# Queries by kv as four float32 products in the quarters of the array, from the fifth chunk on

## The chip, the cores and the metric

The kernel runs on one core of one Trainium2 chip. Its time is the device time of one execution in microseconds (us). Less is better.

## What is computed

Linear attention over 8 batches, 8 heads, 576 tokens and 64 dimensions a head, and a gated feed-forward layer behind it. q is drawn with a spread of 0.8, k with 0.32, v with 0.1.

```python
q_s = exp(q - max(q, axis=-1));  q_s /= sum(q_s, axis=-1) + 1e-9      # over the head's 64 dimensions
k_s = exp(k - max(k, axis=2));   k_s /= sum(k_s, axis=2) + 1e-9       # over the 576 tokens
kv  = einsum('bhsd,bhse->bhde', k_s, v)                               # 64 x 64 for each head
x   = einsum('bhsd,bhde->bhse', q_s, kv)                              # queries by kv
x   = x.transpose(0, 2, 1, 3).reshape(4608, 512)                      # tokens x (heads * 64)
out = ((x @ w_a) * (x @ w_b)) @ w_out                                 # 512 -> 1536 -> 512
```

## The kernel before, in words

The 4608 tokens are worked in nine chunks of 512 (`T`, index `c` from 0). A batch has 576 tokens, so a batch ends within most chunks. While the feed-forward layer of chunk `c` runs on TensorE, the attention of chunk `c + 1` is worked in between. So the queries of the fifth chunk (`c` = 4) are worked during the feed-forward of the fourth.

**Feed-forward.** `x @ w_a` and `x @ w_b` are formed by seven products of blocks instead of eight (Strassen's scheme in Winograd's form). Each float32 operand is split into two float32r parts, high and low, and each product is high by high, high by low and low by high. One call of `product` (L835) issues 12 matmuls of 256 columns into a two-bank tile of PSUM: `kx` (bank pair tag k0), `ky` and later `kp` (tag k1), `ka` (tag k2). VectorE and ScalarE join the results (L1443 to L1481). `project` (L864) multiplies the gated result by `w_out`: 12 matmuls of 512 columns a call, into `po`.

**Attention.** The eight heads are four pairs (`g`); a pair fills the 128 partitions, 64 of each head. For each batch and two pairs, `kv_two` takes the softmax of k times v by plain float32 products (`pk`, L582): each head writes one half of the columns of the array, with all 128 rows; ten products to a pair. Then `kv_two` scales them, masks what is between two heads, and splits the block-diagonal 128 x 128 matrix into two float32r parts `kvh` and `kvl`.

For the queries, `q_stats` takes the maximum and the sum of each token and head, which go through a transposition (`pst`, L686) and through memory and come back as rows along the tokens (`q_rows`, tile `mr`). `q_turned` loads q with its dimensions on the partitions (`qtt`). `q_exp` (L721) adds the maximum's row on VectorE (L722), takes the exponential on ScalarE (L723), and splits it into `qh` on ScalarE (L341) and `ql` on VectorE (L344). `x_product` (L752) multiplies by kv: three float32r products of all 512 columns into one bank (tag `at`), or six where a batch ends within the chunk (L761). VectorE multiplies by the row of the reciprocal sums (L960) and writes `xf`, the input of the feed-forward.

**The order.** Up to the third chunk a table by hand (`ORDER`) gives each engine's order. From there on a scheduler places the instructions, with what `attend` hands it at three calls for each of six pairs of blocks; calls may be pinned behind a named instruction. `attention_tasks` (L914) makes the list of steps that those calls take.

**The end.** `store` (L871) copies each 128 x 512 block of results from PSUM, on VectorE and ScalarE in turn in the last chunk, and SP issues one DMA for each.

Of the kernel before, what the change touches and what calls it, by code (L numbers as in the profile page):

```python
# [7 lines left out]
F32 = mybir.dt.float32  # L8
# [247 lines left out]
def linear_attention_then_gated_ffn(  # L256
# [40 lines left out]
    TT = T // P  # L297
    NCH = NT // T
    LATE = NCH - qt_late.shape[0]

    const = ctx.enter_context(tc.tile_pool(name="const", bufs=1))
    sb = ctx.enter_context(tc.tile_pool(name="sb", bufs=2))
# [35 lines left out]
    def split(hi, lo, src, hi_engine="act"):  # L338

        if hi_engine == "act":  # L340
            nc.scalar.copy(out=hi, in_=src)  # L341
# [273 lines left out]
    def kv_two(b, g, kts, vts, tag):  # L615

        pk = ps.tile([P, 2, D + 1], F32, name="pk", tag=tag)
        for n in range(2):
            kv_sums(kts[n], vts[n], tag, pk[:, n])
        den = sb.tile([P, 2], F32, name="den2")  # L620
        nc.vector.tensor_scalar_add(den, pk[:, :, D], EPS)
        nc.vector.reciprocal(out=den, in_=den)
        kv = sb.tile([P, 2, P], F32, name="kv2", bufs=1)
        for n in range(2):
            nc.vector.scalar_tensor_tensor(
                out=kv[:, n].rearrange("p (h d) -> p h d", h=2),
                in0=pk[:, n, 0:D].unsqueeze(1).broadcast_to([P, 2, D]), scalar=den[:, n:n + 1],
                in1=mask.rearrange("p (h d) -> p h d", h=2), op0=ALU.mult, op1=ALU.mult,
            )
        split(*kv_home(b, g), kv, "dve")  # L630


    wholes = sb.tile([P, 2, NP, P], F32, name="wholes", tag="mr", bufs=2)
# [32 lines left out]

    def q_stats(qt, st):
        qv = qt.rearrange("p j h d -> p h j d")  # L670
        nm, rs = st[:, :, 0], st[:, :, 1]
        nc.vector.tensor_reduce(out=nm, in_=qv, axis=AX.X, op=ALU.max, negate=True)  # L672
        for h in range(2):
            for j in range(TT):
                nc.scalar.activation(  # L675
                    out=qt[:, j, h], in_=qt[:, j, h], func=AF.Exp, bias=st[:, h, 0, j:j + 1],
                    accum_out=st[:, h, 1, j:j + 1],
                )
        nc.vector.tensor_scalar_add(rs, rs, EPS)
        nc.vector.reciprocal(out=rs, in_=rs)  # L680

    def q_stats_out(c, st):

        n = NP * 2 * 2 * TT
        pst = ps.tile([n, P], F32, name="pst", tag="at")
        nc.tensor.transpose(pst, st.rearrange("p g h w j -> p (g h w j)"), ident)  # L686
# [3 lines left out]
        nc.sync.dma_start(out=dq, in_=sst)  # L690
        return dq.rearrange("(g h w j) p -> g h w (j p)", g=NP, h=2, w=2)

    def roomy(c):
        return c > LATE

# [23 lines left out]
    def q_exp(c, qt, rows):  # L721
        nc.vector.tensor_tensor(out=qt, in0=qt, in1=rows[0], op=ALU.add)  # L722
        nc.scalar.activation(out=qt, in_=qt, func=AF.Exp)  # L723
        if roomy(c):
            hl = sb.tile([P, 2, T], F32R, name="qhl", tag="mr", bufs=2)
            qh, ql = hl[:, 0], hl[:, 1]
        else:
            qh = sb.tile([P, T], F32R, name="qh", bufs=1)
            ql = sb.tile([P, T], F32R, name="ql", bufs=1)
        split(qh, ql, qt)  # L730
        return qh, ql
# [10 lines left out]
    def x_whole(c, g, qw, tag):  # L742
# [6 lines left out]
            nc.tensor.matmul(px[:, s], whole[b, g], qw[:, s], start=True, stop=True)  # L749
        return px  # L750

    def x_product(c, g, qhl, tag="at"):  # L752
        qh, ql = qhl
        t0 = c * T
        b0, b1 = t0 // S, (t0 + T - 1) // S
        n0 = min(T, (b0 + 1) * S - t0)
        px = ps.tile([P, T], F32, name="px", tag=tag)
        for b, s in ((b0, slice(0, n0)), (b1, slice(n0, T)))[:b1 - b0 + 1]:
            kvh, kvl = kvs[b, g]
            for i, (w, m) in enumerate(((kvh, qh), (kvh, ql), (kvl, qh))):  # L760
                nc.tensor.matmul(px[:, s], w, m[:, s], start=(i == 0), stop=(i == 2))  # L761
        return px
# [108 lines left out]
    def store(c, po):  # L871
        for t in range(TT):
            ot = sb.tile([P, DM], F32, name="ot", tag="wr", bufs=4)
            if c == NCH - 1 and t % 2 == 0:
                nc.vector.tensor_copy(out=ot, in_=po[t])
            else:
                nc.scalar.copy(out=ot, in_=po[t])
            nc.sync.dma_start(out=out[c * T + t * P:c * T + (t + 1) * P, :], in_=ot)
# [39 lines left out]
    def attention_tasks(c):  # L918

        xfs[c] = sb.tile([P, NP, T], F32, name="xf", bufs=1)  # L920
        steps = key_steps(range(c * T // S, (c * T + T - 1) // S + 1))
        if c == 2:
            steps = [(tasks[8][4],)] + steps
            steps[0] += tuple(lambda g=g: kv_split_whole(1, g) for g in range(NP))
            for g in (1, 2, 3):
                load, soft, turn, back, prod = late_key_task(g, "at")
                steps.append((
                    load, lambda soft=soft, turn=turn: (soft(), turn()),
                    lambda back=back, prod=prod: (back(), prod()),
                ))  # L930
        stats, last, turned, rows = [], [], [], []
        every = {}
        for g in range(NP):
            box = {}

            def a0(g=g, box=box):
                if g == 0:
                    every["st"] = sb.tile([P, NP, 2, 2, TT], F32, name="st", bufs=1)
                box["q"] = q_load(c, g)

            def a1(g=g, box=box):
                q_stats(box["q"], every["st"][:, g])
# [12 lines left out]
            def b1(box=box):  # L955
                box["e"] = q_exp(c, box["q"], box["r"])

            def b2(g=g, box=box):
                px = x_product(c, g, box["e"])
                nc.vector.tensor_tensor(out=xfs[c][:, g], in0=px, in1=box["r"][1], op=ALU.mult)  # L960

            turned.append(t0)
            rows.append(r0)
            last.append((b1, b2) if roomy(c) else (lambda t0=t0, r0=r0: (t0(), r0()), b1, b2))
        stats, steps = pipeline(stats), pipeline(steps)
        seq = []
        for i in range(max(len(stats), len(steps))):
            seq.append((stats[i] if i < len(stats) else []) + (steps[i] if i < len(steps) else []))
        last = pipeline(last)
# [12 lines left out]
        return seq + last  # L982
# [409 lines left out]
    for c in range(1, NCH):  # L1392
# [5 lines left out]
        for n, i in enumerate(pairs):  # L1398
# [53 lines left out]
            if not end:  # L1452
                with part("proj"):
                    run_pending()
            with part("attend"):
                attend(c > 2 and last)
            kp = ps.tile([P, 2, H], F32, name="kp", tag="k1")
            multiply(kp, S1, T1, True)
            multiply(kx, A12, B21, False)
            with part("pair"):  # L1460
                nc.vector.tensor_tensor(out=cc[:, 3], in0=kp, in1=u3, op=ALU.add)  # L1461
                nc.scalar.copy(out=cc[:, 0, 0], in_=kx[:, 0])  # L1462
# [75 lines left out]
```

## Time and profile before

| | |
|---|---|
| time, median of 3 runs | 936.63 us (936.39 to 936.83) |
| time of the profiled execution | 935.81 us |
| its span, first to last instruction | 934.0 us |
| TensorE busy | 924.7 us, 99% |
| VectorE busy | 618.0 us, 66% |
| ScalarE busy | 394.0 us, 42% |
| GpSimd busy | 107.9 us, 12% |
| moved by DMA | 253.27 MB, mean 271 GB/s |

In the profile's rows PE is TensorE's matmuls and PEld its weight loads, DVE is VectorE, ACT ScalarE, POOL GpSimd and SP the engine that issues DMAs. L761 is line 761 of the kernel before. A row of the timeline gives the start, the time from the start of its first to the end of its last instruction, the engine, the line, what is written and read, and how many. Matmuls overlap: the next starts while the last one drains, so the price of one is read from start to start, not from its length. "128\*64" stands for the rows and columns of the array that a matmul uses. A plain float32 product is recorded as two matmuls, a float32r product as one.

### The profile page before, as it was taken

Reading aid. Unit: us, or ns where it says so; the run is one execution under the profiler, and the core shown is the slowest. Engines: PE = TensorE matmul, PEld = TensorE weight load, DVE = VectorE, ACT = ScalarE, POOL = GpSimd, SP = SyncE. Lnnn points to the kernel's source line nnn. Section 1 sums busy time; section 2 is a strip of 40 time slices with the busy share of each in tenths; the row PEclk is TensorE's granted clock in tenths of the full one; section 3 lists DMA queues with packets and bytes.
Section 4 is the critical chain, followed back from the end, with each engine's and each line's share of the span. In section 5 each row is a group of like instructions: output and inputs, shape, how many; then the busy total and the mean of one; then the engine's idle time right before and its main releaser. Section 6 shows DMA issues by size and latency. Waiting matters only on the chain.

```text
span 934.0 us, 17535 instructions
## 1 busy us (share of the span) xinstructions
PE 924.7 (99%) x6565; PEld 835.2 (89%) x6565; DVE 618.0 (66%) x1218; ACT 394.0 (42%) x1094; POOL 107.9 (12%) x88
## 2 busy tenths in 40 slices
PE   8999999999999999999999999999999999999998
PEld 6677789999988999999999999999999999999997
DVE  7998898788854677467656574666657454753433
ACT  8988774435521345133613271324424352322111
POOL 1654434330000000000100010000000000000000
PEclk9999999999999999999999999999999999999999
DMA  9989889989788879983989289945997389627761
GB/s 349 349 308 367 333 321 337 330 310 285 266 305 291 259 270 345 283 330 110 337 255 380 94 302 297 361 169 198 331 320 247 102 293 308 219 96 270 248 224 47
DMA packets 88947, 253.27 MB, mean 271 GB/s; under 512 B 10720, under 2 KB 11296, under 8 KB 88864
## 3 DMA queue, kind: packets, MB, share of 16 engines
q1 hardware_dynamic: 88864, 252.16, 78.5%
q8 instruction: 52, 0.85, 0.4%
q14 instruction: 31, 0.25, 0.1%
HBM read 213.09 MB, written 36.93 MB: 268 GB/s over the span
## 4 chain that ended last, share of the span: by engine, by line
PE 95%; DVE 2%; DMA 1%; ACT 0%; POOL 0%; issue 0%; SPq 0%; DVEq 0%; POOLq 0%
PE po L864 31%; PE kx L835 14%; PE kp L835 14%; PE ka L835 14%; PE pt L805 7%; PE ky L835 7%; PE px L761 2%; PE pk L582 2%; PE po L850 1%; PE px L749 1%; DMA kt_first<-in_kt 1%; DVE xo L344 0%; POOL mx L512 0%; DVE kt L544 0%; DVE mc L1128 0%
## 5 line engine op out<-in xcount | busy, mean ns | idle before, releaser
L864 PE MATMUL po<-wo_w,gh 128*128 128x512 f32 x840 | 264.5, 396 | 0.0
L835 PE MATMUL kx<-xo,ws 128*128 128x256 f32 x1152 | 184.7, 282 | 0.3 <-DVE cc L1463 0.2
L835 PE MATMUL ka<-xo,ws 128*128 128x256 f32 x1152 | 177.7, 282 | 0.7 <-DVE u L1447 0.4
L835 PE MATMUL kp<-xo,ws 128*128 128x256 f32 x1152 | 174.8, 283 | 0.5 <-DVE cc L1461 0.5
L864 PEld LDWEIGHTS po<-wo_w,gh 128*128 128x128 f32 x840 | 151.3, 188 | 25.1 <-ACT gh L341 0.5
L835 PEld LDWEIGHTS kx<-xo,ws 128*128 128x128 f32 x1152 | 160.7, 189 | 6.7 <-DVE cc L1463 0.7
L835 PEld LDWEIGHTS ka<-xo,ws 128*128 128x128 f32 x1152 | 157.9, 189 | 6.7 <-issue 0.6
L835 PEld LDWEIGHTS kp<-xo,ws 128*128 128x128 f32 x1152 | 155.7, 189 | 5.8 <-DVE cc L1461 0.8
L864 PE MATMUL po<-wo_w,gl 128*128 128x512 f32 x420 | 153.0, 396 | 0.0
L341 ACT CAST gh<-cc 128x512 fp32r<-128x512 f32 x96 | 58.6, 620 | 168.8 <-DVE cc L1475 145.4
L1462 ACT COPY cc<-kx 128x256 f32<-128x256 f32 x48 | 17.8, 372 | 177.6 <-PE kx L835 170.4
L864 PEld LDWEIGHTS po<-wo_w,gl 128*128 128x128 f32 x420 | 78.0, 188 | 15.7 <-DVE gl L344 0.4
L1474 DVE TENSOR_TENSOR cc<-kp,u 128x512 f32<-128x512 f32 x48 | 33.1, 690 | 86.0 <-PE kp L835 85.9
L805 PE MATMUL pt<-xo,ws 128*128 128x512 f32 x288 | 87.0, 418 | 0.0
L835 PE MATMUL ky<-xo,ws 128*128 128x256 f32 x576 | 86.6, 281 | 0.0
L675 ACT ACTIVATE qt<-qt,st 128x64 f32<-128x64 f32 x224 | 75.3, 340 | 19.6 <-DVE st L672 18.7
L835 PEld LDWEIGHTS ky<-xo,ws 128*128 128x128 f32 x576 | 76.8, 189 | 1.1
L344 DVE TENSOR_TENSOR gl<-cc,gh 128x512 fp32r<-128x512 f32 x96 | 67.1, 704 | 12.9 <-ACT gh L341 12.8
L1461 DVE TENSOR_TENSOR cc<-kp,u 128x512 f32<-128x512 f32 x48 | 33.2, 691 | 62.7 <-PE kp L835 62.2
L805 PEld LDWEIGHTS pt<-xo,ws 128*128 128x128 f32 x288 | 52.9, 188 | 17.3 <-issue 4.2
L512 POOL PARTITION_ALL_REDUCE mx<-m x20 | 18.1, 910 | 433.0 <-DVE m L523 433.0
L1443 ACT COPY u<-kx 128x512 f32<-128x512 f32 x48 | 28.0, 583 | 51.5 <-PE kx L835 48.0
(150 smaller groups left out, 1117.3 us busy)
## 6 DMA issues: line engine op xcount, KB each, us to landing
ws<-dw SPq DMA_DIRECT2D x260, 512.0 KB, 6.0
dw<-ws SPq DMA_DIRECT2D x42, 512.0 KB, 6.6
mr<-dq SPq DMA_DIRECT2D x112, 128.0 KB, 6.0
raw<-in_w_ab SPq DMA_DIRECT2D x24, 512.0 KB, 7.8
out<-ot SPq DMA_DIRECT2D x36, 256.0 KB, 4.7
vt<-in_v SPq DMA_DIRECT2D x28, 325.0 KB, 6.1
qt<-in_q SPq DMA_DIRECT2D x32, 256.0 KB, 5.1
kt<-in_k SPq DMA_DIRECT2D x24, 320.0 KB, 5.3
```

What stands on the lines that cost most here:

```text
L341: nc.scalar.copy(out=hi, in_=src)
L344: return nc.vector.tensor_tensor(out=lo, in0=src, in1=hi.bitcast(F32), op=ALU.subtract)
L512: nc.gpsimd.partition_all_reduce(out_ap=mx, in_ap=kv_max(kt), channels=P, reduce_op=bass_isa.ReduceOp.max,)
L582: nc.tensor.matmul(pk[h * D:(h + 1) * D], kt[:, j, h], vt[:, j, h], start=(j == 0), stop=(j == J - 1),)
L675: nc.scalar.activation(out=qt[:, j, h], in_=qt[:, j, h], func=AF.Exp, bias=st[:, h, 0, j:j + 1], accum_out=st[:, h, 1, j:j + 1],)
L761: nc.tensor.matmul(px[:, s], w, m[:, s], start=(i == 0), stop=(i == 2))
L805: nc.tensor.matmul(pt, w[:, wp], x[g][:, xp], start=(g == 0 and i == 0), stop=(g == NP - 1 and i == 2),)
L835: ins = nc.tensor.matmul(pt[:, n], w[:, n, wp, c], x[:, xp, c], start=(first and n == 0 and i == 0), stop=(i == 5), skip_group_check=True,)
L864: ins = nc.tensor.matmul(po[t], a[:, ts], wo[f][:, w], start=(f == ends[0] and i == 0), stop=(f == ends[1] and i == 2),)
L1443: nc.scalar.copy(out=u2, in_=kx)
L1461: nc.vector.tensor_tensor(out=cc[:, 3], in0=kp, in1=u3, op=ALU.add)
L1474: nc.vector.tensor_tensor(out=cc[:, 1], in0=kp, in1=u2, op=ALU.add)
```

## The change

From the fifth chunk on (`c >= WHOLE`, with `WHOLE = 4`) the queries by kv are plain float32 products and nothing of them is split. The host lays out q for these chunks so that the two halves of a chunk's tokens (256 each) lie on the two halves of the partitions, with the two heads one behind the other along the columns. kv is kept whole, as float32, on both halves of the partitions. A pair of heads then has four products of 64 rows by 64 columns and 256 tokens, one in each quarter of the array; the two row halves write two different banks, `at` and a second one that is free at that place (`spare`: k1 at the second of three calls, k0 at the third and first). Where a batch ends within a half, its products are cut in two. `kv_again` adds the two split parts of the batch that both kinds of chunk use. In `attend`'s list for these chunks, loads, exponentials and products are given to calls 7 to 14. In the feed-forward, the second group of `kx` comes ahead of `kp` instead of behind it. In the last store the last block is copied in two halves, one by VectorE and one by ScalarE, with a DMA for each.

```diff
@@ kv_two
+        if b * S >= WHOLE * T:
+            kv_whole_home(b, g)
+            for h in range(2):
+                own = slice(h * D, (h + 1) * D)
+                for rows in (slice(0, D), slice(D, P)):
+                    nc.vector.tensor_tensor(
+                        out=kv_parts[b, g // 2][rows, :, own], in0=pk[own, :, 0:D],
+                        in1=den[own].unsqueeze(2).broadcast_to([D, 2, D]), op=ALU.mult,
+                    )
+            return
@@ q_exp
+        if c >= WHOLE:
+            return qt
         if roomy(c):
             hl = sb.tile([P, 2, T], F32R, name="qhl", tag="mr", bufs=2)
@@
+    def x_whole_halves(c, g, qt):
+
+        t0 = c * T
+        edge = (t0 // S + 1) * S - t0
+        px = [ps.tile([P, H], F32, name=f"px{n}", tag=tag) for n, tag in enumerate(("at", at["spare"]))]
+        parts = []
+        for n in range(2):
+            cut = min(max(edge - n * H, 0), H)
+            parts.append([(n, lo, hi) for lo, hi in ((0, cut), (cut, H)) if hi > lo])
+        for n, lo, hi in [p[0] for p in parts] + [p[1] for p in parts if len(p) > 1]:
+            rows = slice(n * D, (n + 1) * D)
+            kv = kvs[(t0 + n * H + lo) // S, g]
+            for h in range(2):
+                own = slice(h * D, (h + 1) * D)
+                nc.tensor.matmul(
+                    px[n][own, lo:hi], kv[rows, own], qt[rows, h * H + lo:h * H + hi],
+                    start=True, stop=True,
+                )
+        return px
+
     def x_product(c, g, qhl, tag="at"):
+        if c >= WHOLE:
+            return x_whole_halves(c, g, qhl)
@@ store
+            if c == NCH - 1 and t == TT - 1:
+                rows = out[c * T + t * P:c * T + (t + 1) * P, :]
+                nc.vector.tensor_copy(out=ot[:, 0:H], in_=po[t][:, 0:H])
+                nc.sync.dma_start(out=rows[:, 0:H], in_=ot[:, 0:H])
+                nc.scalar.copy(out=ot[:, H:T], in_=po[t][:, H:T])
+                nc.sync.dma_start(out=rows[:, H:T], in_=ot[:, H:T])
+                continue
@@ attention_tasks
+                if c >= WHOLE:
+                    for n in range(2):
+                        half = slice(n * H, (n + 1) * H)
+                        nc.vector.tensor_tensor(
+                            out=xfs[c][:, g, half], in0=px[n], in1=box["r"][1][:, half], op=ALU.mult
+                        )
+                    return
                 nc.vector.tensor_tensor(out=xfs[c][:, g], in0=px, in1=box["r"][1], op=ALU.mult)
...
         if c > 3:
-            begin = 3 * NI - 3 - len(last) - 2
-            seq += [[] for _ in range(len(seq), begin)]
-            for g in range(NP):
-                seq[begin + g:begin + g + 1] = [rows[g:g + 1] + turned[g:g + 1]]
-            for n, now in enumerate(last):
-                seq[begin + n + 2:begin + n + 3] = [(seq[begin + n + 2] if n + 2 < NP else []) + now]
+            seq += [[] for _ in range(len(seq), 3 * NI - 3)]
+            for g, n in enumerate((10, 11, 13, 14)):
+                load, (exp, mul) = rows[g:g + 1] + turned[g:g + 1], every["last"][g]
+                seq[n - 3] = seq[n - 3] + load
+                seq[n - 1] = seq[n - 1] + [exp]
+                seq[n] = [mul] + seq[n]
@@ the feed-forward's loop
+            at["spare"] = "k1"
             with part("attend"):
                 attend(c > 2 and last)
+            if c + 1 >= WHOLE:
+                multiply(kx, A12, B21, False)
             kp = ps.tile([P, 2, H], F32, name="kp", tag="k1")
             multiply(kp, S1, T1, True)
-            multiply(kx, A12, B21, False)
+            if c + 1 < WHOLE:
+                multiply(kx, A12, B21, False)
...
+            at["spare"] = "k0"
             with part("attend"):
                 attend(c > 2 and last)
```

Three places in the engines' order follow. A row gives the line, the operation, what is written and read, the columns of the array by the columns streamed, and how many stand together.

TensorE before, where the fifth chunk's first pair is worked (`px` the queries by kv, `po` the projection, `kp`, `ka`, `kx` the feed-forward):

```order
L864 MATMUL po_4279<-wo_w,gl_4748 128x512
L761 MATMUL px<-qhl,kvh_3144 128x256 x2
L761 MATMUL px<-qhl,kvl_3145 128x256
L761 MATMUL px<-qhl,kvh_4320 128x256 x2
L761 MATMUL px<-qhl,kvl_4321 128x256
L835 MATMUL kp<-xo,ws 128x256 x12
L835 MATMUL ka<-xo,ws 128x256 x12
```

TensorE now, the first two pairs (each number of `px` is one bank; rows of the projection's other blocks are left out):

```order
L815 MATMUL px_4834<-qtt,kvw_4133 64x256 x2
L815 MATMUL px_4835<-qtt,kvw_4385 64x256 x2
L906 MATMUL kx<-xo,ws 128x256 x5
...
L935 MATMUL po_4272<-wo_w,gl_4766 128x512
L906 MATMUL ka<-xo,ws 128x256 x2
L815 MATMUL px_4897<-qtt,kvw_4133 64x256 x2
L906 MATMUL ka<-xo,ws 128x256 x2
L906 MATMUL kp<-xo,ws 128x256 x12
L815 MATMUL px_4898<-qtt,kvw_4385 64x256 x2
```

The first pair's four products stand together; the second pair's two halves stand apart, with two `ka` and twelve `kp` between them. The third pair is like the second, and of the fourth pair's products the last stands behind twelve `kp`. It is so in all five chunks: seven places each.

TensorE before, where kv of the fifth chunk's new batch is summed in the fourth chunk, its second group (`pk`):

```order
L835 MATMUL kp<-xo,ws 128x256 x12
L835 MATMUL kx<-xo,ws 128x256 x6
L582 MATMUL pk<-vt,kt 64x65 x20
L835 MATMUL kx<-xo,ws 128x256 x2
L835 MATMUL ky<-xo,ws 128x256 x12
```

And now:

```order
L906 MATMUL kx<-xo,ws 128x256 x12
L583 MATMUL pk<-vt,kt 64x65 x10
L906 MATMUL ky<-xo,ws 128x256 x12
L906 MATMUL ka<-xo,ws 128x256 x12
L906 MATMUL kx<-xo,ws 128x256
L583 MATMUL pk<-vt,kt 64x65 x10
```

The twenty products stand in two groups of ten. The first group of that batch is split in the same way; the later batches' groups stay whole.

VectorE before, at the ninth chunk's first pair (`xf` takes px, `qhl` is the low part of q, `cc` and `u` the feed-forward's sums):

```order
L1461 TENSOR_TENSOR cc<-kp,u_9346 128x512
L1464 TENSOR_TENSOR cc<-cc 128x256
L722 TENSOR_TENSOR qtt<-qtt,mr_9347 128x512
L1463 TENSOR_TENSOR cc<-kx,cc 128x256
L344 TENSOR_TENSOR qhl<-qtt,qhl 128x512
L960 TENSOR_TENSOR xf<-px,mr_9294 128x512
L1474 TENSOR_TENSOR cc<-kp,u_9345 128x512
```

VectorE now:

```order
L1535 TENSOR_TENSOR u_9344<-ka,u_9343 128x512
L769 TENSOR_TENSOR qtt<-qtt,mr_9291 128x512
L1043 TENSOR_TENSOR xf<-px_9404,mr_9239 128x256
L1043 TENSOR_TENSOR xf<-px_9405,mr_9239 128x256
L1555 TENSOR_TENSOR cc<-kx,cc 128x256
L1553 TENSOR_TENSOR cc<-kp,u_9344 128x512
```

px's bank pair is read by two rows ahead of what joins `kx` and `kp`; the row that made q's low part is gone.

More of the change, by code (lines that the diff above doesn't have):

```diff
@@ L299, in linear_attention_then_gated_ffn @@
     LATE = NCH - qt_late.shape[0]
+    WHOLE = 4
     const = ctx.enter_context(tc.tile_pool(name="const", bufs=1))
@@ L630, in kv_two, with kv_whole_home, kv_again @@
         split(*kv_home(b, g), kv, "dve")
+    def kv_whole_home(b, g, tag="kvh"):
+        q = g // 2
+        kv_parts[b, q] = kv = sb.tile([P, 2, P], F32, name=f"kvw{q}", tag=f"{tag}{q}")
+        for n in (2 * q, 2 * q + 1):
+            kvs[b, n] = kv[:, n % 2]
+    def kv_again(b):
+        for g in range(0, NP, 2):
+            kvh, kvl = kv_parts[b, g // 2]
+            kv_whole_home(b, g, "kvl")
+            for h in range(2):
+                own = slice(h * D, (h + 1) * D)
+                for rows in (slice(0, D), slice(D, P)):
+                    nc.vector.tensor_tensor(
+                        out=kv_parts[b, g // 2][rows, :, own], in0=kvh.bitcast(F32)[own, :, own],
+                        in1=kvl.bitcast(F32)[own, :, own], op=ALU.add,
+                    )
     wholes = sb.tile([P, 2, NP, P], F32, name="wholes", tag="mr", bufs=2)
@@ L665, in q_soft_first, with q_stats @@
         return qt
-    def q_stats(qt, st):
+    def q_stats(qt, st, whole_q):
         qv = qt.rearrange("p j h d -> p h j d")
-        nm, rs = st[:, :, 0], st[:, :, 1]
-        nc.vector.tensor_reduce(out=nm, in_=qv, axis=AX.X, op=ALU.max, negate=True)
+        if whole_q:
+            w = st.rearrange("p h w j -> p (h w j)")
+            nm, rs = w[:, 0:2 * TT], w[:, 2 * TT:4 * TT]
+            nh = nm.rearrange("p (a h j) -> p h a j", a=2, h=2)
+            for h in range(2):
+                nc.vector.tensor_reduce(
+                    out=nh[:, h], in_=qt[:, :, h].rearrange("p (a j) d -> p a j d", a=2),
+                    axis=AX.X, op=ALU.max, negate=True,
+                )
+            rh = rs.rearrange("p (h j) -> p h j", h=2)
+        else:
+            nm, rs = st[:, :, 0], st[:, :, 1]
+            rh = rs
+            nc.vector.tensor_reduce(out=nm, in_=qv, axis=AX.X, op=ALU.max, negate=True)
         for h in range(2):
             for j in range(TT):
+                at_j = nh[:, h, j // 2, j % 2:j % 2 + 1] if whole_q else nm[:, h, j:j + 1]
                 nc.scalar.activation(
-                    out=qt[:, j, h], in_=qt[:, j, h], func=AF.Exp, bias=st[:, h, 0, j:j + 1],
-                    accum_out=st[:, h, 1, j:j + 1],
+                    out=qt[:, j, h], in_=qt[:, j, h], func=AF.Exp, bias=at_j,
+                    accum_out=rh[:, h, j:j + 1],
                 )
@@ L750, in x_whole @@
         return px
+    def x_whole_halves(c, g, qt):
[9 more added lines that the diff above has]
+            kv = kvs[(t0 + n * H + lo) // S, g]
+            for h in range(2):
+                own = slice(h * D, (h + 1) * D)
+                nc.tensor.matmul(
+                    px[n][own, lo:hi], kv[rows, own], qt[rows, h * H + lo:h * H + hi],
+                    start=True, stop=True,
+                )
+        return px
     def x_product(c, g, qhl, tag="at"):
+        if c >= WHOLE:
+            return x_whole_halves(c, g, qhl)
         qh, ql = qhl
@@ L930, in attention_tasks @@
                 ))
+        if c == WHOLE and c * T % S:
+            steps = [(lambda: kv_again(c * T // S),)] + steps
         stats, last, turned, rows = [], [], [], []
@@ L941, in a1 @@
             def a1(g=g, box=box):
-                q_stats(box["q"], every["st"][:, g])
+                q_stats(box["q"], every["st"][:, g], c >= WHOLE)
                 if g == NP - 1:
@@ L959, in b2 @@
                 px = x_product(c, g, box["e"])
+                if c >= WHOLE:
+                    for n in range(2):
+                        half = slice(n * H, (n + 1) * H)
+                        nc.vector.tensor_tensor(
+                            out=xfs[c][:, g, half], in0=px[n], in1=box["r"][1][:, half], op=ALU.mult
+                        )
+                    return
                 nc.vector.tensor_tensor(out=xfs[c][:, g], in0=px, in1=box["r"][1], op=ALU.mult)
@@ L968, in attention_tasks @@
             seq.append((stats[i] if i < len(stats) else []) + (steps[i] if i < len(steps) else []))
+        every["last"] = last
         last = pipeline(last)
         if c > 3:
-            begin = 3 * NI - 3 - len(last) - 2
-            seq += [[] for _ in range(len(seq), begin)]
-            for g in range(NP):
-                seq[begin + g:begin + g + 1] = [rows[g:g + 1] + turned[g:g + 1]]
-            for n, now in enumerate(last):
-                seq[begin + n + 2:begin + n + 3] = [(seq[begin + n + 2] if n + 2 < NP else []) + now]
+            seq += [[] for _ in range(len(seq), 3 * NI - 3)]
[4 more added lines that the diff above has]
+                seq[n] = [mul] + seq[n]
             return seq
@@ L1516 @@
     qlate = q.transpose(0, 2, 1, 3).reshape(b * s // T, T, g, 2 * d)[2:].transpose(0, 2, 3, 1)
+    qhalf = qlate.reshape(-1, g, 2, d, 2, T // 2).transpose(0, 1, 4, 3, 2, 5).reshape(qlate.shape)
+    qlate = np.concatenate([qlate[:2], qhalf[2:]])
     wab = np.stack([w.view(np.int64).reshape(2, dm // P // 2, P, df // P // 2, 2, P) for w in (w_a, w_b)])
```

1 line of the change is left out of this document (added).

## Prediction

> **What bounds the kernel now.** I read the page's busy times first, then its chain, then TensorE's waits, then the busy time by stage. The profiled execution took 935.81 us for a span of 934.0 us; the median of the three runs shown is 936.63 us. A sum made on the trace therefore goes onto 935.8 us and, for the forecast, onto 936.6 us. What a measurement of this kernel can tell from no change is about 0.2%, 1.9 us.
>
> The page: the span, each engine's busy share, and the chain that ended last.
>
> ```profile
> span 934.0 us, 17535 instructions
> PE 924.7 (99%) x6565; PEld 835.2 (89%) x6565; DVE 618.0 (66%) x1218; ACT 394.0 (42%) x1094; POOL 107.9 (12%) x88
> PE 95%; DVE 2%; DMA 1%; ACT 0%; POOL 0%; issue 0%; SPq 0%; DVEq 0%; POOLq 0%
> ```
>
> TensorE's waits (total, times, longest), its largest and the one at the products to be changed:
>
> ```profile
> PE pq L1196 <- DVE den L590: 1.4, 1, 1.4
> PE px L761 <- ACT qhl L341: 0.3, 1, 0.3
> ```
>
> Stretches of the late chunks (length, then busy time of TensorE, its weight loads, VectorE and ScalarE):
>
> ```profile
> 325.00:424.00 99.00, 99.00 (x760) 92.18 (x759) 68.44 (x137) 38.18 (x114) 3.80 (x4) 1.00 0.90 307
> 722.00:821.00 99.00, 99.00 (x687) 92.03 (x686) 56.41 (x107) 36.11 (x111) 0.00 (x0) 1.00 0.69 226
> ```
>
> Where the change acts, TensorE has work in every microsecond at the full clock (1.00) and nothing waits. So there is only one account: what the change adds to or takes from TensorE's stream counts in full, and what it takes from VectorE and ScalarE counts nothing.
>
> **Products taken out (px, from the fifth chunk on).** The next rows are TensorE's timeline at one pair of heads of each chunk from the fifth to the ninth: start, length, group. The first row is px's first group, the next what follows px.
>
> ```profile
> 398.84 0.39 PE L761 MATMUL px<-qhl,kvh 128*128 128x256 f32 x2
> 399.55 1.12 PE L835 MATMUL kp<-xo,ws 128*128 128x256 f32 x8
> ...
> 501.92 0.46 PE L761 MATMUL px<-qhl,kvh 128*128 128x320 f32 x2
> 502.68 1.25 PE L835 MATMUL kx<-xo,ws 128*128 128x256 f32 x9
> 503.76 0.52 PE L835 MATMUL ky<-xo,ws 128*128 128x256 f32 x3
> ...
> 601.41 0.51 PE L761 MATMUL px<-qhl,kvh 128*128 128x384 f32 x2
> 602.21 1.40 PE L835 MATMUL kx<-xo,ws 128*128 128x256 f32 x10
> 603.45 0.76 PE L835 MATMUL ky<-xo,ws 128*128 128x256 f32 x5
> ...
> 697.04 0.56 PE L761 MATMUL px<-qhl,kvh 128*128 128x448 f32 x2
> 697.89 1.68 PE L835 MATMUL kp<-xo,ws 128*128 128x256 f32 x12
> 699.41 0.28 PE L835 MATMUL ka<-xo,ws 128*128 128x256 f32 x1
> ...
> 794.15 0.62 PE L761 MATMUL px<-qhl,kvh 128*128 128x512 f32 x2
> 794.84 0.52 PE L835 MATMUL ka<-xo,ws 128*128 128x256 f32 x3
> ```
>
> From start to start px takes 0.71, 0.76, 0.80, 0.85 and 0.69 us. The price of an ordinary product comes from twelve kp followed by kx:
>
> ```profile
> 788.87 1.58 PE L835 MATMUL kp<-xo,ws 128*128 128x256 f32 x12
> 790.28 1.23 PE L835 MATMUL kx<-xo,ws 128*128 128x256 f32 x9
> ```
>
> 1.41 / 12 = 0.1175 us for 256 columns; px's three products of 512 columns in 0.69 us make 0.23 us each. Behind px the next group runs a little late: 9 kx in 1.08 us instead of 1.06, 10 in 1.24 instead of 1.18, 12 kp in 1.52 instead of 1.41. That belongs to px too: 0.02, 0.06 and 0.11 us. Each chunk has four pairs: 4 x (3.81 + 0.19) = 16.0 us taken out.
>
> **Products put in.** Before shows no product in a quarter of the array. Nearest are the plain float32 products pk (L582) in two column halves, 128 rows by 64 columns. Two of their groups, of 40 and of 20 records (each product is recorded as two passes), with what surrounds them:
>
> ```profile
> 667.45 1.35 PE L835 MATMUL kx<-xo,ws 128*128 128x256 f32 x10
> 668.73 1.39 PE L582 MATMUL pk<-vt,kt 128*64 128x65 f32 x40
> 670.05 0.50 PE L835 MATMUL kx<-xo,ws 128*128 128x256 f32 x2
> 670.39 1.55 PE L835 MATMUL ky<-xo,ws 128*128 128x256 f32 x12
> ...
> 188.86 0.40 PE L835 MATMUL ka<-xo,ws 128*128 128x256 f32 x2
> 189.19 0.80 PE L582 MATMUL pk<-vt,kt 128*64 128x65 f32 x20
> 189.92 0.73 PE L864 MATMUL po<-wo_w,gh 128*128 128x512 f32 x2
> 190.49 0.28 PE L835 MATMUL kp<-xo,ws 128*128 128x256 f32 x1
> ```
>
> The ten kx would be through at 667.45 + 1.175 = 668.62, and ky's start less two kx is 670.155: 40 records cost 1.53 us. Likewise 20 records cost 190.49 - 0.46 - (188.86 + 0.235) = 0.935 us. The difference gives 0.030 us per record, and 0.34 us remain per group, whatever its length: going into halves and coming back. The price of a plain float32 pass in the whole array:
>
> ```profile
> 17.78 1.02 PE L749 MATMUL px<-qw,wholes 128*128 128x512 f32 x2
> 18.64 0.60 PE L1196 MATMUL pq<-ident,qts 128*128 128x128 f32 x4
> ```
>
> Two passes of 512 columns in 0.86 us: 0.84 ns per column, so 0.215 us for 256 and 0.055 us for 65. pk pays 0.030 for 65, so its two halves do run side by side.
>
> A half of the tokens is now two products in two column quarters: four passes of 0.215, two at a time, 0.43 us. With two passes in each of four quarters, all four side by side would also take 0.43; only two at a time, 0.86. By the order, each chunk's px stands in seven places: one with all eight passes (first pair), four of one half each, one with six passes and one with two (the last pair's last product stands behind twelve kp; where a batch ends within the chunk the pieces differ, with the same columns in all). I take four side by side, since in pk each half keeps its pace beside the other: 7 x (0.43 + 0.34) = 5.39 us a chunk, 27.0 in five. Two at a time: 0.86 x 3 + 0.645 + 0.43 + 2.38 = 6.03 a chunk, 30.2.
>
> The Trainium skill prices this otherwise: in the page "TensorE: Matmul & The Clock Gate", section "Measured speedup vs the span model", packed tiles take one product's time plus about 4 ns per further tile, with no term for entering or leaving. By that rule the sum would lack every 0.34, and it is a rival below.
>
> **Products torn apart.** In two places of the fourth chunk the order splits pk's group of 20 products into two of 10. Each split pays the switch again: 2 x 0.34 = 0.7 us.
>
> **VectorE, ScalarE, queues.** These go, or change:
>
> ```profile
> L341 ACT CAST qhl<-qtt 128x512 fp32r<-128x512 f32 x24 | 14.9, 620 | 0.6
> L960 DVE TENSOR_TENSOR xf<-px,mr 128x512 f32<-128x512 f32 x28 | 19.3, 689 | 24.5 <-PE px L761 19.2 <-DMA ws<-dw 3.8 <-DMA kt<-in_k 0.9
> L1463 DVE TENSOR_TENSOR cc<-kx,cc 128x256 f32<-128x256 f32 x48 | 20.1, 419 | 11.9 <-ACT cc L1462 11.7
> ```
>
> Twenty casts of 0.62 us and as many subtractions go; each multiplication of 0.69 us becomes two of about 0.42 (the 256-wide row). VectorE, 56 to 68 of 99 us busy, and ScalarE do not end TensorE's work: nothing gained. The second bank adds a wait: kp (bank k1) or kx (k0) may only start when VectorE has read px's second half, and all TensorE work queues behind it. In the first place of the order 5 kx, 12 po and 4 ka come between, 0.6 + 2.8 + 0.5 = 3.9 us, against 0.84 us for the two halves. I take nothing; without the cover it is at most about 0.8 us a pair. The loads of q and its rows are issued two calls ahead of their use; a call is a fifteenth of 99 us, so 13 us. I take nothing there either, for SP only passes them by weight loads that are prefetched.
>
> **The last store.** The last copy and the four issues of the last chunk:
>
> ```profile
> 929.03 2.32 SPq L878 DMA_DIRECT2D out<-ot  x4
> ...
> 930.40 0.58 ACT L877 COPY ot<-po 128x512 f32<-128x512 f32 x1 [0.81 <-PE po L864]
> ```
>
> The halves can be copied by two engines in about 0.4 us, 0.2 earlier, but a fifth issue stands in SP's line; 2.32 / 4 bounds it by 0.6 us. Between -0.2 and +0.4: I take nothing.
>
> **The sum.** 27.0 - 16.0 + 0.7 = +11.7 us: 947.5 us against the profiled execution, 948.3 us against the median.
>
> **Rivals.**
> Two quarters at a time: pk never shows more than two at once. 30.2 - 16.0 + 0.7 = +14.9: 951.5 us.
> Passes in strict order: a product's two passes need the same quarter, so the second must wait, and what stands behind it waits too. A half then takes three turns of 0.215 instead of two, the eight passes five, the six passes four: (4 x 1 + 3 + 2) x 0.215 = 1.94 a chunk, 9.7 in all. In pk the extra turn of 0.055 would then be part of the 0.34, which takes back 37 x 0.055 = 2.0. Together +19.4: 956 us. The Trainium skill has this rule in the same page, section "The mechanism": products start and end in program order. pk's 0.030 cannot tell, as long groups hide the ends.
> The switch is not paid in quarters (the other side). For it speaks pst, also 64 columns wide:
>
> ```profile
> 763.94 0.28 PE L835 MATMUL kp<-xo,ws 128*128 128x256 f32 x1
> 764.06 0.27 PE L686 MATMUL pst<-ident,st 128*64 128x128 f32 x1
> 764.09 1.19 PE L835 MATMUL kp<-xo,ws 128*128 128x256 f32 x8
> ```
>
> Eight kp would take 0.28 + 7 x 0.1175 = 1.10, so pst costs 0.03 + 0.09 = 0.12 us and no 0.34. Against it: pst is one transposition that uses all rows, and pk pays each time. Without the switch: 15.1 - 16.0 = -0.9: 935.7 us, no difference. It decides below 0.9 / 35 = 0.03 us a place.
> Half the switch, where draining is hidden by long passes: 37 x 0.17 - 0.9 = +5.4: 942 us.
> The bank's wait is not covered: 20 x 0.2 more on top, 952 us.
>
> **How the numbers follow.** The forecast, full switch and four quarters, 0.45; two at a time 0.17; strict order 0.10; half a switch 0.09; the bank's wait 0.03; no switch 0.13; a gain whose cause I do not see 0.03. The time is the forecast's, 948.3 us. From 941 to 957 us leaves out no switch and the unseen gain (0.16) and some strict order above (0.03). No switch gives -0.9 us, mostly no difference, in part a gain with the store's 0.2 and shorter ends: faster 0.05, same 0.11, slower 0.84.
>
> **What the profile after would show.** Right: seven groups of px a chunk, each with about 0.34 us beside its passes; eight passes in 0.43 + 0.34; TensorE busy as before in the late chunks, which are about 2.3 us longer each; VectorE and ScalarE less busy. Wrong: px's groups as short as their passes (no switch), an 8-pass group near 1.2 us (two at a time) or 1.4 (strict order), or TensorE idle ahead of kp or kx with VectorE as releaser.

## The result, and the profile after

| | before | after |
|---|---|---|
| median of 4 runs each, us | 936.73 (936.39 to 937.22) | 948.89 (948.64 to 951.77) |
| ratio, 95% interval | | 1.0136 (1.0116 to 1.0156) |
| the profiled execution, us | 935.81 | 948.91 |
| its span, us | 934.0 | 947.1 |

Between the medians the kernel became 12.2 us slower (1.30%); 948.3 was forecast. The ratio in the table is that of the means, which one run of after at 951.77 us raises. The page of after, in the order of before's: the span, the engines, the chain that ended last.

```profile
span 947.1 us, 17745 instructions
PE 937.5 (99%) x6665; PEld 830.2 (88%) x6665; DVE 608.4 (64%) x1247; ACT 383.2 (40%) x1074; POOL 105.6 (11%) x88
PE 95%; DVE 3%; DMA 1%; ACT 0%; issue 0%; POOL 0%; SPq 0%; DVEq 0%; POOLq 0%
```

VectorE and ScalarE have 9.6 and 10.8 us less to do, and the span is 13.1 us longer. TensorE is as full as before; its stream has grown. In the first of the two late stretches shown of before, still at the full clock (1.00):

```profile
325.00:424.00 99.00, 98.98 (x732) 87.45 (x731) 63.08 (x142) 33.58 (x105) 3.44 (x4) 1.00 0.87 294
```

**The px places.** TensorE's timeline of after at three of the seven px places of the fifth chunk: one with eight passes (first pair), one with four, and one with two. Columns: start, length, line, output and input, tile, moved columns, count.

```profile
396.10 0.40 PE L935 MATMUL po<-wo_w,gl 128*128 128x512 f32 x1
396.42 0.66 PE L815 MATMUL px<-qtt,kvw 64*64 64x256 f32 x8
397.01 0.86 PE L906 MATMUL kx<-xo,ws 128*128 128x256 f32 x5
397.71 0.62 PE L935 MATMUL po<-wo_w,gh 128*128 128x512 f32 x2
...
400.49 0.40 PE L906 MATMUL ka<-xo,ws 128*128 128x256 f32 x2
400.82 0.65 PE L815 MATMUL px<-qtt,kvw 64*64 64x256 f32 x4
401.40 0.50 PE L906 MATMUL ka<-xo,ws 128*128 128x256 f32 x2
401.74 1.59 PE L906 MATMUL kp<-xo,ws 128*128 128x256 f32 x12
...
419.87 1.68 PE L906 MATMUL kp<-xo,ws 128*128 128x256 f32 x12
421.49 0.64 PE L815 MATMUL px<-qtt,kvw 64*64 64x256 f32 x2
422.06 1.58 PE L906 MATMUL ka<-xo,ws 128*128 128x256 f32 x11
423.48 1.60 PE L906 MATMUL kp<-xo,ws 128*128 128x256 f32 x12
```

The first po (0.235 us a product, as the prediction has it) would be through at 396.335; the five kx, 0.59 us, would have to start at 397.71 - 0.59 = 397.12 to end where the next po starts. So the place costs 0.79 us. The four-pass place: 401.74 - 0.235 - (400.49 + 0.235) = 0.78. The two-pass place, worked out alike from the starts of its single neighbours: 0.77. Eight passes cost what two cost: four quarters run side by side, and a place costs 0.43 us of passes and 0.34 to 0.37 besides, whatever it holds. Over all 35 places the same working, from the starts of the single products, gives 27.3 us, where before's px cost 16.0.

These rows also show what the 0.35 consists of. Ahead of px TensorE starts 0.085 us late (396.42 against 396.335). Inside, from 396.42 to 397.01, stand 0.59 us for two passes of 0.215, so 0.16 more. Behind it five kx take 0.70 us instead of 0.59, so 0.11 more. The weight loads (PEld) of the same place tell why:

```profile
395.87 0.19 PEld L935 LDWEIGHTS po<-wo_w,gl 128*128 128x128 f32 x1
396.42 0.21 PEld L815 LDWEIGHTS px<-qtt,kvw 64*64 64x64 f32 x8 [0.37 <-issue]
397.01 0.65 PEld L906 LDWEIGHTS kx<-xo,ws 128*128 128x128 f32 x5 [0.39 <-issue]
```

An ordinary load starts a whole product ahead of its own: po's at 395.87, for the product at 396.10. Those of px and of the kx behind px start with their products. What they wait for isn't a semaphore ("issue"). It looks like a drain: the array must be empty first (0.085 us in, about as much out), and then the new load stands open (about 0.05 us for 64 columns, 0.11 for 128). The experiments below test this. The Trainium skill names the drain in the page "TensorEngine Tiling (Array Packing)", section "Key Properties": changing the tiling mode, not just the tile, drains TensorE. The trace agrees, in that these loads start no earlier than their products, and adds the price of about 0.35 us.

**The keys' products (pk).** One of the fourth chunk's four groups of 20 records in after, and one of the two groups of 40 in before:

```profile
362.28 1.34 PE L906 MATMUL kp<-xo,ws 128*128 128x256 f32 x10
363.55 0.80 PE L583 MATMUL pk<-vt,kt 128*64 128x65 f32 x20
364.28 1.19 PE L935 MATMUL po<-wo_w,gl 128*128 128x512 f32 x4
```

```profile
370.30 1.39 PE L582 MATMUL pk<-vt,kt 128*64 128x65 f32 x40
371.61 0.50 PE L835 MATMUL kx<-xo,ws 128*128 128x256 f32 x2
```

From pk's start to the next: twice 0.73 against once 1.31, so 0.15 more for the split, and 0.2 more outside these rows (0.09 ahead, 0.11 behind, as at px). With the neighbours' starts the four groups cost 0.92 to 0.93 each, 3.7 us, and the two of before 3.0: +0.7.

**What else moved.** TensorE's waits of after hold none for px in quarters (L815), and none of its products waits on px's second bank. One stands at kp, which uses that bank (k1), but it is no work of the change: it starts at 264.09 us, ahead of every px in quarters, and before has the same wait at 262.80. The row of after, then that of before:

```profile
PE kp L906 <- DVE cc L1553: 0.5, 1, 0.5
```

```profile
PE kp L835 <- DVE cc L1461: 0.5, 1, 0.5
```

Two short waits of the weight loads in the fourth chunk are new in after:

```profile
340.67 0.66 PEld L906 LDWEIGHTS ky<-xo,ws 128*128 128x128 f32 x5 [0.21 <-DVE cc L1567]
```

```profile
357.83 0.90 PEld L906 LDWEIGHTS kx<-xo,ws 128*128 128x128 f32 x7 [0.21 <-ACT u L1531]
```

Each of the two delays TensorE by 0.27 to 0.28 us (two starts later than at 0.1175 a product), 0.55 together; by the engines named they wait for a bank to be read, in a chunk whose px is unchanged.

A part of the difference lies ahead of everything that was changed. The transposition pst that stands at 264.62 us, ahead of the first products that differ, in before, in after, and in a kernel told below (e7) that differs from before only from the fifth chunk on:

```profile
264.62 0.27 PE L686 MATMUL pst<-ident,st 128*64 128x128 f32 x1
```

```profile
265.91 0.27 PE L731 MATMUL pst<-ident,st 128*64 128x128 f32 x1
```

```profile
265.93 0.27 PE L686 MATMUL pst<-ident,st 128*64 128x128 f32 x1
```

After is 1.29 us later there, and so is the unchanged code of e7. The early chunks come out differently from one profiled execution to the next (in e5, which has after's code there, pst starts at 264.66), and before's was an early one: 0.9 us under its median.

So the 13.1 us between the two traces are 1.3 of such scatter, 27.3 - 16.0 = 11.3 at px, 0.7 at pk, 0.55 of new short waits, and some 0.7 less spread over the other products, which no row accounts for.

**The last store.** The end of after:

```profile
943.52 0.42 DVE L947 COPY ot<-po 128x256 f32<-128x256 f32 x1
943.98 0.37 ACT L949 COPY ot<-po 128x256 f32<-128x256 f32 x1 [1.27 <-DVE ot L947]
```

ScalarE's half did not run beside VectorE's but behind it: its row names the first half's copy as what it waited for. From TensorE's last start to the span's end are 4.03 us, and 4.06 before.

### The profile page after: what moved, and what is told of

The parts are those of the page before. It is cut to its first block, busy times and chain, and to the rows that moved or that the text cites. A ratio compares the mean times of both kernels' runs of the same rounds, so it can differ in the third digit from the quotient of the medians.

```text
span 947.1 us, 17745 instructions
## 1 busy us (share of the span) xinstructions
PE 937.5 (99%) x6665; PEld 830.2 (88%) x6665; DVE 608.4 (64%) x1247; ACT 383.2 (40%) x1074; POOL 105.6 (11%) x88
## 4 chain that ended last, share of the span: by engine, by line
PE 95%; DVE 3%; DMA 1%; ACT 0%; issue 0%; POOL 0%; SPq 0%; DVEq 0%; POOLq 0%
PE po L935 30%; PE kx L906 14%; PE kp L906 14%; PE ka L906 14%; PE pt L876 7%; PE ky L906 7%; PE px L815 2%; PE pk L583 2%; PE po L921 1%; PE warm L332 1%; PE px L798 1%; PE px L832 1%; DMA ws<-dw 1%; DVE xo L345 0%; POOL mx L513 0%
## 5 line engine op out<-in xcount | busy, mean ns | idle before, releaser
L906 PE MATMUL kx<-xo,ws 128*128 128x256 f32 x1152 | 181.3, 283 | 0.3 <-DVE cc L1555 0.2
L906 PE MATMUL kp<-xo,ws 128*128 128x256 f32 x1152 | 172.5, 283 | 0.7 <-DVE cc L1553 0.5
L906 PEld LDWEIGHTS kx<-xo,ws 128*128 128x128 f32 x1152 | 158.2, 189 | 8.8 <-issue 3.1
L935 PE MATMUL po<-wo_w,gl 128*128 128x512 f32 x420 | 150.7, 397 | 0.0
L513 POOL PARTITION_ALL_REDUCE mx<-m x20 | 16.0, 807 | 441.6 <-DVE m L524 441.6
```

The costliest lines, as they stand in the source:

```text
L906: ins = nc.tensor.matmul(pt[:, n], w[:, n, wp, c], x[:, xp, c], start=(first and n == 0 and i == 0), stop=(i == 5), skip_group_check=True,)
L935: ins = nc.tensor.matmul(po[t], a[:, ts], wo[f][:, w], start=(f == ends[0] and i == 0), stop=(f == ends[1] and i == 2),)
```

## The experiments

The theory: every place of products in small tiles among whole-array products pays about 0.35 us for going in and coming out, and the place's passes run in all four quarters at once. The main rivals: the quarters are slow in themselves; the cost belongs to plain float32 and not to the tile; it belongs to what else was changed.

### e1: eight passes in one place where the order allows it

```diff
-        for n, lo, hi in [p[0] for p in parts] + [p[1] for p in parts if len(p) > 1]:
+        chain = []
+        for n, lo, hi in parts[1] + parts[0]:
...
-                nc.tensor.matmul(
+                chain.append(nc.tensor.matmul(
...
+        behind_each_other(chain)
```

The same products on the same data, in 25 places instead of 35.

> The changed kernel, with a pair's second half given out first and all its products chained, so that a pair's four products stand together in all places but the last pair's: 25 places instead of 35, the same products. Switch theory (0.34 us a place whatever it holds, four quarters side by side): three places of eight passes at 0.80 and two of 0.78 a chunk, 3.96 x 5 = 19.8 us against 27.5, so 7.7 us less than the changed kernel, 941.2 us. If only two quarters run at a time: the joined places take 1.2 us, nothing is gained beyond 10 x 0.34 = 3.4 less what the joined passes queue up, about 948. If the loss lies in the float32 passes and not in the places: no change, 948.9 us.

Measured: 942.56 us (941.70 to 944.35) against 936.83 for before on that chip, ratio 1.0061 (1.0045 to 1.0076): 6.4 us of the loss are gone, with ten places fewer, where 7.7 had been expected. In its trace the 25 places cost 19.1 us, 8.2 less than after's 35, so the places gave at least what was expected. But the same trace has two waits for weight loads that after's late chunks lack (`ka`, for `ws`: 1.07 us at 401.58 and 0.17 at 602.07), and these take 1.2 back in that execution. Two of the places, with four and with eight passes:

```profile
518.54 0.40 PE L937 MATMUL po<-wo_w,gl 128*128 128x512 f32 x1
518.87 0.33 PE L816 MATMUL px<-qtt,kvw 64*64 64x64 f32 x4
519.13 1.71 PE L908 MATMUL kp<-xo,ws 128*128 128x256 f32 x12
520.76 0.66 PE L816 MATMUL px<-qtt,kvw 64*64 64x192 f32 x8
```

Here the four passes of one place have only 64 columns each, and the place costs 0.47 us; places of four passes with 128, 192 and 256 columns cost 0.57, 0.68 and 0.78. That is a straight line: 2 x 0.80 ns a column, and 0.37 us at no columns. Eight passes of which each quarter gets 256 columns cost 0.80. The fixed part does not shrink with long passes, which is against the half-switch rival.

### e5: two pairs in one place

```diff
+                    held_q.append((g, box))
+                    if len(held_q) < 2:
+                        return
+                    px = x_whole_halves(c, [g for g, _ in held_q], [box["e"] for _, box in held_q])
...
-        px = [ps.tile([P, H], F32, name=f"px{n}", tag=tag) for n, tag in enumerate(("at", at["spare"]))]
+        px = [ps.tile([P, 2, H], F32, name=f"px{n}", tag=tag) for n, tag in enumerate(("at", at["spare"]))]
```

Two pairs' halves fill one bank, so that the two banks hold two pairs; 10 places instead of 35, chained as in e1.

> The changed kernel, with the products of two pairs of heads in one place: each bank holds one row half's result of both pairs side by side, so that a chunk has two places of sixteen passes instead of seven. Switch theory: 0.34 + 4 x 0.215 = 1.20 us a place, 2.4 a chunk, 12.0 us against 27.5 in the changed kernel and 16.0 in the kernel before: 15.5 us less than the changed one, 933.4 us, which is 3.3 us under the kernel before. Passes theory (the loss is in the float32 passes): no change, 948.9 us. Bank theory (the second bank's reading holds TensorE): the two banks are now read by four multiplications, 1.7 us, so TensorE is seen idle ahead of kp or kx and the time lies above 936.

Measured: 934.23 us (933.07 to 935.51, 6 runs), ratio 0.9969 (0.9958 to 0.9981): 14.7 us less than after and 2.6 less than before.

```profile
400.06 0.52 PE L907 MATMUL ka<-xo,ws 128*128 128x256 f32 x3
400.51 1.09 PE L817 MATMUL px<-qtt,kvw 64*64 64x256 f32 x16
401.53 1.70 PE L907 MATMUL kp<-xo,ws 128*128 128x256 f32 x12
403.06 0.64 PE L907 MATMUL ka<-xo,ws 128*128 128x256 f32 x4
```

The place costs 403.06 - 12 x 0.1175 - (400.06 + 3 x 0.1175) = 1.24 us for sixteen passes, four deep: 4 x 0.215 = 0.86, and 0.38 for the place. The ten places cost 12.6 us, about 3.5 less than before's px. This decides the question: the quarters aren't slow, the number of places is what costs.

### e2: the same plain float32 in the whole array

```diff
+            chain.append(nc.tensor.matmul(px[:, s], kvs[b, g], qt[:, s], start=True, stop=True).ins)
```

kv block-diagonal in float32, 128 rows by 128 columns, 512 tokens, one bank: no small tiles, twice the passes' time.

> The changed kernel with its float32 products in the whole array: kv block-diagonal, q laid out as before, two passes of 512 columns into one bank, nothing split, no quarters. Switch theory: 0.86 us a pair and no price for the place, 20 x 0.86 = 17.3 us against 27.5: 10.2 us less than the changed kernel, 938.7 us. Passes theory: the whole array needs as much or more, so 948 us or above.

Measured: 939.37 us (938.69 to 940.52, 7 runs), ratio 1.0027 (1.0017 to 1.0038).

```profile
395.07 0.39 PE L920 MATMUL po<-wo_w,gl 128*128 128x512 f32 x1
395.30 1.03 PE L802 MATMUL px<-qtt,kvw 128*128 128x256 f32 x4
395.97 0.94 PE L891 MATMUL kx<-xo,ws 128*128 128x256 f32 x5
396.75 0.87 PE L891 MATMUL kp<-xo,ws 128*128 128x256 f32 x6
```

px starts on time (395.305), and the place costs 396.75 - 0.59 - 395.305 = 0.86 us: four passes of 0.215 and nothing beside them. Plain float32 has no entry price; the tile has. So after's passes alone do save time (0.43 against 0.86 us a pair), and it is given back 35 times.

### e3 and e4: the last store, and the order of kx and kp

e3 takes the store of before again; e4 puts kp ahead of kx again in the late chunks.

> The changed kernel with the last block copied and stored whole, as before. By the forecast the halves gave nothing: 948.9 us within 0.3. If the halved store shortens the end, 0.2 to 0.6 us more; if the fifth issue lengthens it, as much less.

> The changed kernel with kp ahead of the second kx group, as before. Bank theory: kp then stands right behind px's second bank, and TensorE waits for VectorE, 0.3 to 0.8 us a pair, 6 us or more above the changed kernel. Forecast (the cover is there either way, since the order keeps the projection in between): 948.9 us within 1.

Measured: e3 949.55 us (948.55 to 950.49), ratio 1.0133 (1.0120 to 1.0147); e4 949.54 (947.47 to 950.52), ratio 1.0130 (1.0111 to 1.0150), against 1.0136 for after. Neither part of the change moves the time by as much as these intervals, over 1 us either way, can tell. In e3's trace 4.04 us lie behind TensorE's last start, against 4.03 in after, and e4's trace shows no wait of TensorE's products in the late chunks.

### e7, e8, e9, e10: the price of one tiny product, by its tile

The kernel before, with a plain float32 product of 16 columns ahead of each of the 20 px from the fifth chunk on. The four kernels differ in its tile alone; its result is overwritten. In 15 of the 20 places px follows at once; in five, those of the rows below, the tiny product stands alone ahead of `ky`.

```diff
+            chain.append(nc.tensor.matmul(px[0:D, 0:16], ident[0:D, 0:D], ident[0:D, 0:16], start=True, stop=True).ins)
```

That is e7, a quarter of 64 x 64; e8 has ident (128 x 128), e9 ident[0:D] (64 rows, 128 columns), and e10 ident[:, 0:D] (128 rows, 64 columns).

> The kernel before, with one more plain float32 product of 16 columns in one quarter of the array (64 rows by 64 columns) directly ahead of each px from the fifth chunk on; px overwrites it. It adds 20 places and next to no columns (two passes of 16 columns, 0.03 us). Switch theory: 20 x (0.34 + 0.03) = 7.4 us, 944.1 us. If quarters have no price for the place: 20 x 0.03 to 0.1, 937.3 to 938.7 us.

> The control to the tiny product in a quarter: the same 16 columns ahead of each px, but in the whole array (128 rows by 128 columns). Switch theory: no switch, two short passes whose weight loads of 128 columns may show, 20 x 0.05 to 0.25, 937.7 to 941.7 us. If any added plain float32 product costs the same: as long as the tiny product in a quarter.

> The same 16 columns ahead of each px, now in a row half (64 rows by 128 columns). If halving the rows alone is a switch too: about 0.34 us a place as in a quarter, 20 x 0.37 = 7.4 us, 944.1 us. If only the halving of the columns is: as the control in the whole array.

> The kernel before with a 16-column plain float32 product of 128 rows by 64 columns ahead of each of the twenty px from the fifth chunk on (its result is overwritten). In the traces the same product costs 0.21 us a place in the whole array, 0.41 in a quarter and 0.52 in a row half. Theory of the drain (the load of a smaller tile is not begun beside the pass before it, and the whole array's load behind it neither): 0.09 for the pass before to be out, two loads of 0.053, two passes of 0.013, 0.09 again, 0.107 for the whole array's load: 0.42 us a place, as the quarter, 946 us. Rival (columns do not matter, only rows do: pst, 128 rows by 64 columns, has its load beside the pass before it): only the second load and the load behind show, 0.05 + 0.107 = 0.16 us a place, about 941 us.

| tile of the tiny product | us, median | before there | ratio (95%) | us a place, in the trace |
|---|---|---|---|---|
| e8, whole 128 x 128 | 942.56 | 936.43 | 1.0059 (1.0042 to 1.0075) | 0.22 |
| e7, quarter 64 x 64 | 946.04 | 936.43 | 1.0094 (1.0079 to 1.0109) | 0.41 |
| e10, 128 rows, 64 columns | 945.66 | 936.41 | 1.0096 (1.0081 to 1.0111) | 0.41 |
| e9, 64 rows, 128 columns | 947.75 | 936.43 | 1.0115 (1.0098 to 1.0132) | 0.52 |

The last column is px with the tiny product less px alone, over the twenty places. The first three came out slower than I had expected (944.1 for e7, 937.7 to 941.7 for e8, 944.1 or e8's price for e9). For e7 and e9 part of this is the place: 0.41 and 0.52 us against 0.37, since I had left out the open loads. e8's 0.22 lies within the 0.05 to 0.25 expected. The rest is not at the places: twenty of them make 4.4, 8.2, 8.2 and 10.3 us in the table's order, and the medians rise by 1.0 to 1.7 more. In all four traces 4.97 to 4.99 us lie between TensorE's last start and the span's end, where before's has 4.06: the last two stores take 3.0 to 3.1 us to land instead of 2.0. Why they do is open. The loads show what the places consist of. First the whole array (e8), TensorE and its loads:

```profile
487.70 1.12 PE L840 MATMUL kx<-xo,ws 128*128 128x256 f32 x8
488.66 0.29 PE L760 MATMUL px<-ident 128*128 128x16 f32 x2
```

```profile
488.54 0.32 PEld L760 LDWEIGHTS px<-ident 128*128 128x128 f32 x2
488.77 1.14 PEld L840 LDWEIGHTS ky<-xo,ws 128*128 128x128 f32 x9
```

The first load begins 0.12 us ahead of its pass, beside the last kx, and px starts when the eight kx are through (488.64). Only the second load and ky's stay open, since 16 columns hide neither: 2 x 0.107 = 0.21. Now the quarter (e7):

```profile
488.49 1.11 PE L840 MATMUL kx<-xo,ws 128*128 128x256 f32 x8
489.54 0.29 PE L760 MATMUL px<-ident 64*64 64x16 f32 x2
```

```profile
489.54 0.19 PEld L760 LDWEIGHTS px<-ident 64*64 64x64 f32 x2
489.75 1.00 PEld L840 LDWEIGHTS ky<-xo,ws 128*128 128x128 f32 x8
```

The kx are through at 489.43, but the load does not begin before 489.54. Loads that hide behind nothing follow each other at 0.053 us for 64 columns and 0.107 for 128 in this trace. So the place is 0.09 for the drain, twice a load of 0.053 and a pass of 0.013, 0.09 again, and 0.107 for ky's load: 0.42 us. The row half (e9) has the same, with loads of 128 columns that last twice as long (from its first pass to the next load 0.32 us instead of 0.21):

```profile
489.95 0.29 PEld L760 LDWEIGHTS px<-ident 64*128 64x128 f32 x2
490.27 1.01 PEld L840 LDWEIGHTS ky<-xo,ws 128*128 128x128 f32 x8
```

With that account I expected 0.42 us a place, about 946 us, for the column half (e10), against 941 if only the rows mattered. It took 945.66, and 0.41 a place; the time agrees so well in part by luck, since some 0.9 us of it stand at the end and not at the places. Its loads are those of the quarter:

```profile
489.72 0.19 PEld L760 LDWEIGHTS px<-ident 128*64 128x64 f32 x2
489.94 1.01 PEld L840 LDWEIGHTS ky<-xo,ws 128*128 128x128 f32 x8
```

So rows or columns, each of the three smaller tiles tried for a plain float32 product costs the way in and the way out. Products of other types were not tried in them.

### e6: two pairs, and pk's groups joined again

```diff
-        for n in range(2):
-            kv_sums(kts[n], vts[n], tag, pk[:, n])
+        chain = []
+        for n in (1, 0) if b * S >= WHOLE * T else (0, 1):
+            kv_sums(kts[n], vts[n], tag, pk[:, n], chain)
+        if b * S >= WHOLE * T:
+            behind_each_other(chain)
```

e5 with the fourth chunk's four groups of 20 records put together to two of 40.

> The two-pairs version with one thing more: the keys' products of the fourth chunk stand again in two places of twenty instead of four of ten. Theory (each place of small tiles among whole-array products costs about 0.35 us for going in and coming out): two places fewer, 0.7 us less than the two-pairs version, which stood 2.6 us below the kernel before on its chip: about 3.3 us below before, 933.3 us if before is at 936.6, with an error of about 0.5. Rival (the splitting cost nothing and the 0.70 us seen in the trace comes back elsewhere): 2.6 us below before, 934.0 us.

Measured: 934.79 us (933.35 to 940.32, 12 runs), ratio 0.9986 (0.9972 to 1.0001). This is inconclusive. In the trace the two groups cost 1.51 us each again, so the 0.7 are gone there, but the runs scatter over 7 us, and e5's over 2.4. The profiled execution (939.01 us) shows one cause of scatter, a wait for a weight load and what follows it. First the wait, then two stretches of that time, with TensorE's granted clock third from the right:

```profile
PE kx L912 <- DMA ws<-dw: 2.3, 1, 2.3
```

```profile
491.60:494.20 2.60, 0.31 (x3) 0.10 (x1) 1.74 (x3) 0.63 (x1) 0.00 (x0) 1.00 1.02 231
494.20:497.80 3.60, 3.55 (x13) 3.10 (x14) 0.00 (x0) 0.00 (x0) 0.00 (x0) 0.55 1.00 316
```

Joining pk is not needed for such a wait: e1's trace has it with 1.07 us, and e2's has one of 0.48 us at kx (691.39), both without that edit. e5's one trace has none; whether more runs of it would is open. The version shown to beat both kernels is e5.

## Why the prediction was right

**The switch, 0.34 us a place: right.** It was read off pk, whose groups of 40 and 20 records left 0.34 us at no records. At px it is 0.34 to 0.37, whether the place holds two passes or twelve. What the prediction didn't know is its make: two drains of about 0.09 us, an open load of 0.05 and one of 0.11 (e7 to e10).

**Four quarters side by side: right.** 0.79 us for eight passes, where 0.77 was forecast, 1.2 by two at a time and 1.4 by strict order. The Trainium skill's rule that products start and end in program order ("TensorE: Matmul & The Clock Gate", section "The mechanism") did not lead to the turns that the rival made of it: eight passes cost what two do. The starts here say nothing against the rule itself.

**px's sum: right.** 27.0 put in and 16.0 taken out were forecast; 27.3 and 16.0 were measured. "About 2.3 us longer each" is 11.3 / 5 = 2.3.

**pk torn apart: right.** +0.7 forecast, +0.7 measured.

**No switch, the rival on the other side: wrong.** Its evidence, pst, stands: this 64-column transposition has its load beside the product before it, 0.10 us ahead of its own start (763.96 against 764.06), and pays no drain. But it doesn't carry over to a product in 64 columns, as e10 shows; what sets a transposition apart was not tried. The span model of the Trainium skill ("Measured speedup vs the span model", the same page), with about 4 ns a tile and no term for going in or out, agrees with the inside of a place, where eight passes in four tiles took 0.79 us and two passes in one tile 0.77; among whole-array products it lacks 0.35 us.

**The bank's wait, taken at nothing: right.** No product waited for px's second half; the one wait at kp stands in before too. In e4, with the other order, none of the late chunks waits either, so the order of kx and kp is not what kept the wait away. The two short waits of 0.27 us in the fourth chunk were not foreseen.

**VectorE's and ScalarE's relief, taken at nothing: right.** Some 10 us each, and TensorE is as full as before. Whether the 0.7 us that no row accounts for come from it is not shown.

**The store, taken at nothing: right, for a reason of its own.** The gain of 0.2 needed the two halves copied at the same time; they ran in turn, and the end is as long as in e3 (4.03 and 4.04 us).

**The whole.** +11.7 forecast, 12.2 measured between medians. px and pk, the two terms of the sum, are 12.0 in the traces. The 0.55 of short waits, which the sum lacks, and the 0.7 that no row accounts for go opposite ways; that they nearly cancel is luck. That the traces differ by more (13.1) comes from before's early execution.

## What to carry to other kernels

Count the places at which TensorE goes from the whole array into smaller tiles, not only the passes: each costs about 0.35 us here, as much as three ordinary products of 256 columns, whatever plain float32 product is done there. Small tiles pay when a place holds enough to win it back; here a pair's px took 0.80 us in before (16.0 / 20) and takes 0.43 in quarters, so with one pair a place the gain of 0.37 is just eaten up, and with two it shows. If a scheduler sets the order, chain the tiled products, and look for a place's neighbours in the order as it was made.

## What the runs showed of the hardware that was not expected

- The open load at a change of tile depends on the tile's columns and not on its rows: from the first pass to the next kind's load are 0.21 us with 64 x 64, 0.22 with 128 x 64, and 0.32 with 64 x 128.
- A 16-column plain float32 product in the whole array costs 0.22 us though its passes last 0.013 each: its second load and the load behind it find nothing to hide behind. e2's places with a piece of 64 columns cost 0.97 us instead of 0.86; that this has the same reason was not tried.
- In e6, a wait of 2.3 us was followed by a granted clock of 0.55 over the next 3.6 us. By an estimate, that stretch does 3.6 x 0.55 = 2.0 us of work, so the wait cost about 2.3 + 1.6 = 3.9 us in all.
